# A gated recurrence followed by a PReLU network: attention rebuilt with two batches a step and two masked score products

## The chip, the cores and the metric

The kernel runs on one core of one Trainium2 chip. A core has a matrix engine (PE, which loads a stationary operand, PEld, and streams a moving one past it), a vector engine (DVE), an activation engine (ACT), a general engine (POOL), and a queue for transfers (SP); ACT can issue transfers too. Operands lie in on-chip memory (SBUF, 128 partitions), matrix results in PSUM (128 partitions, eight banks of 512 float32 words each). The metric is the device time of one execution in microseconds (us), the median of the runs shown.

## What is computed

Four batches, eight heads, 768 tokens, 48 dimensions a head. A state of 48 x 48 per head decays by a gate for each key dimension and takes in an outer product at each token; the query reads it. The result, with heads side by side (3072 tokens x 384), goes through a network with 2048 hidden units. Everything is float32; the weights arrive as float64.

```python
f = 1.0 / (1.0 + np.exp(-f_logit))
for t in range(S):
    state = f[:, :, t, :, None] * state + np.einsum('bhd,bhe->bhde', k[:, :, t], v[:, :, t])
    y[:, :, t] = np.einsum('bhd,bhde->bhe', q[:, :, t], state)
x = y.transpose(0, 2, 1, 3).reshape(B * S, H * D)
h = x @ w_in
out = (np.maximum(h, 0.0) + alpha * np.minimum(h, 0.0)) @ w_out
```

## The kernel before

The recurrence is worked in chunks of C = 128 tokens of one batch: 4 x 6 = 24 calls of `attention`. A head's dimensions lie on partitions, two heads at 0 and 64 ("par" 0 and 1), four such pairs (HP) beside each other, tokens along the free dimension. Loads of f, q, k and v have three buffers each (L117, L120).

Within a chunk the scores between tokens s and t need q and k with the product of the gates between them. The kernel goes through seven levels (half sizes h = 1 to 64, the loop at L130). At each, VectorE forms G[h]: k of the lower half of each block with the gates up to the block's border (L139), q of the upper half with the gates from the border on (L134), and doubles the running products R and P (L140, L142). `ks` (L153), transposed on PE (pk, L156) and copied by ACT (L158), times V gives the chunk's share of the next state (pd, L163; L172 and L174).

The levels 64 and 32 are whole blocks of scores (pb, L183 and L189), copied by ACT into the score matrix AT. The six others (MASKED: 16, 8, 4, 2, 1 and the diagonal) are computed as whole 32 x 32 diagonal blocks, six products for each of four blocks and eight heads, 192 matmuls a chunk (pa, L208). VectorE multiplies them by masks (pr, L212), POOL adds the six up (sm, L217 and L218, AT, L221). py (L228) is AT by V; L235 adds qs by the old state. ACT copies py to x (L238), PE transposes it (px, L242), ACT copies it into xT (L244).

After each second chunk `network` is called for the pair before: xT is 256 tokens wide. For each of eight pairs of 128 hidden units six matmuls fill one bank (ph, L254, two "net" banks); ACT makes relu(h) and relu(-h) (L259, L260), VectorE joins them with alpha into g (L263, twelve buffers). Then 16 matmuls for each 128 tokens make po (L269), which VectorE copies to o (L272) and SP stores (L274). A float32 matmul shows as two records of PE and two of PEld, a transpose as one.

`load_weights` turns float64 words into float32 on VectorE, seven operations on each of 16 pieces of 384 words (three buffers, transfers on ACT's queue) of w_in and as many of w_out, between the first calls of `attention`.

The program is unrolled; the order on each engine comes from a planner that lists operations by their place in the program and by estimated times. Each engine then keeps its listed order and waits on semaphores. A buffer that a later tile reuses makes its writer wait for the last reader.

Of the kernel before, what the change touches and what calls it, by code (L numbers as in the profile page):

```python
# [14 lines left out]
WP = 384   # weights of a piece, on each partition  # L15
C = 128   # tokens of a chunk
DB = 32   # diagonal blocks whose levels are cut out by masks
MASKED = (16, 8, 4, 2, 1, 0)   # half sizes of these levels; 0 is the diagonal itself
# [3 lines left out]
def kernel(  # L22
# [32 lines left out]
    T = 2 * C   # tokens of a step of the network  # L55
    NG = len(MASKED) // 2
# [3 lines left out]
    ps2 = ctx.enter_context(tc.tile_pool(name="ps2", bufs=2, space=bass.MemoryType.PSUM))  # L60
    ps1 = ctx.enter_context(tc.tile_pool(name="ps1", bufs=2, space=bass.MemoryType.PSUM))

    def pair(name):
        return ps2.tile([128, 2, 512], F32, tag="pair", name=name)

    def bank(name, tag="att"):
        return ps1.tile([128, 512], F32, tag=tag, name=name)
# [3 lines left out]
    msk = const.tile([128, 2, NG * DB], F32, tag="msk", name="msk")  # L71
    nalpha = const.tile([128, NF], F32, tag="nalpha", name="nalpha")
# [3 lines left out]
    nc.scalar.dma_start(out=msk, in_=masks)  # L76
    nc.scalar.dma_start(out=nalpha, in_=alpha)
    nc.vector.tensor_scalar(nalpha, nalpha, -1.0, None, ALU.mult)

    def load_weights(dst, src, name):  # L80
        """float64 words to float32: mantissa times power of two, each with its bits put together."""
        flat = dst.rearrange("p a n -> p (a n)")
        for n in range(0, flat.shape[1], WP):
            raw = work.tile([128, WP, 2], I32, tag="pr", name=f"{name}_raw{n}", bufs=3)
# [3 lines left out]
            # Mantissa: one and its upper 20 bits as an integer, and the lower 32 behind them.  # L88
            mi = work.tile([128, WP], I32, tag="pos", name=f"{name}_mi{n}")
# [3 lines left out]
            # Exponent: from 11 bits to 8. What float32 can't hold becomes zero or infinite.  # L93
            e = work.tile([128, WP], I32, tag="neg", name=f"{name}_e{n}")
# [6 lines left out]
    # Scores of a chunk, tokens s on partitions, t along the free dimension. What lies under the  # L101
    # diagonal stays zero.
    AT = [const.tile([128, 2, HP, C], F32, tag=f"AT{i}", name=f"AT{i}") for i in range(2)]
    for t in AT:
        nc.gpsimd.memset(t, 0.0)

# [3 lines left out]
    def halves(t, h):  # L110
        return t.rearrange("p a (n two h) -> p (a n) two h", two=2, h=h)

    def attention(b, c, state, xT):
        i = f"{b}_{c}"
        ld = {}
        for nm, src in (("f", fT), ("q", qT), ("k", kT)):
            ld[nm] = work.tile([128, HP, C], F32, tag=nm, name=f"{nm}_{i}", bufs=3)  # L117
            nc.sync.dma_start(out=ld[nm], in_=src[b, c])
        q, k = ld["q"], ld["k"]
        vt = work.tile([128, DM], F32, tag="v", name=f"v_{i}", bufs=3)  # L120
        nc.sync.dma_start(out=vt, in_=v[b, c])

        P = work.tile([128, HP, C], F32, tag="P", name=f"P_{i}")
        nc.scalar.activation(P, ld["f"], AF.Sigmoid)
        R = work.tile([128, HP, C], F32, tag="R", name=f"R_{i}")
        nc.gpsimd.memset(R, 1.0)  # L126

        G = {}
        h = 1
        while h < C:  # L130
            G[h] = work.tile([128, HP, C], F32, tag=f"G{h}", name=f"G{h}_{i}")
            g, qh, kh, p, r = (halves(x, h) for x in (G[h], q, k, P, R))
            n = HP * C // (2 * h)
            nc.vector.tensor_tensor(g[:, :, 1], qh[:, :, 1], p[:, :, 1], ALU.mult)  # L134
            if h == 1:
                nc.scalar.copy(g[:, :, 0], kh[:, :, 0])
                nc.scalar.copy(r[:, :, 0], p[:, :, 1])  # L137
            else:
                nc.vector.tensor_tensor(g[:, :, 0], kh[:, :, 0], r[:, :, 0], ALU.mult)  # L139
                nc.vector.tensor_tensor(  # L140
                    r[:, :, 0], r[:, :, 0], p[:, :, 1, h - 1:h].broadcast_to((128, n, h)), ALU.mult)
            nc.vector.tensor_tensor(  # L142
                p[:, :, 1], p[:, :, 1], p[:, :, 0, h - 1:h].broadcast_to((128, n, h)), ALU.mult)
            h *= 2
        qs = work.tile([128, HP, C], F32, tag="qs", name=f"qs_{i}")
        nc.vector.tensor_tensor(qs, q, P, ALU.mult)

        # The chunk's share of the state behind it: k with the decay to the chunk's end, by V.
        last = c == NC - 1
        new_state = None  # L150
        if not last:
            ks = work.tile([128, HP, C], F32, tag="ks", name=f"ks_{i}")
            nc.vector.tensor_tensor(ks, k, R, ALU.mult)  # L153
            pk = bank(f"pk_{i}")
            for hp in range(HP):
                nc.tensor.transpose(pk[:, hp * 128:(hp + 1) * 128], ks[:, hp], ident)  # L156
            ksn = work.tile([128, HP, 128], F32, tag="ksn", name=f"ksn_{i}")
            nc.scalar.copy(ksn.rearrange("p a d -> p (a d)"), pk)  # L158
            pd = bank(f"pd_{i}")
            for hp in range(HP):  # L160
                for par in range(2):
                    hd = 2 * hp + par
                    nc.tensor.matmul(  # L163
                        pd[64 * par:64 * par + 64, hp * D:(hp + 1) * D],
                        lhsT=ksn[:, hp, 64 * par:64 * par + 64], rhs=vt[:, hd * D:(hd + 1) * D],
                        start=True, stop=True)
# [74 lines left out]
        for kt in range(NK):  # L241
            nc.tensor.transpose(px[:, kt * 128:(kt + 1) * 128], x[:, kt * 128:(kt + 1) * 128], ident)  # L242
# [52 lines left out]
def _level_masks():  # L295
# [4 lines left out]
    per = []  # L300
# [46 lines left out]
```

## Time and profile before

| quantity | us |
|---|---|
| median of 3 runs (1087.6 to 1100.94) | 1090.46 |
| span of the profiled execution, first to last instruction | 1085.6 |
| lowest run, the nearest that is given to the profiled execution's own time | 1087.6 |
| PE busy / PEld busy | 828.5 / 644.5 |
| DVE busy | 572.1 |
| ACT busy / POOL busy | 202.3 / 159.8 |

The span is 2.0 us under the lowest run and 4.9 us under the median. Busy times of engines overlap, so they don't add up to the span; a matmul's end is modelled, and records of PE overlap each other. The granted clock of PE, mean 0.817 of full speed, changes between stretches of the run. "Idle before, releaser" names what ended an engine's idle time; "issue" is time in which an engine waited for nothing that the profile shows.

### The profile page before, as it was taken

To read this page: it belongs to the slowest core of one execution; us is meant where nothing else is said; L and a number is where in the kernel's file an instruction comes from. 1 tells how busy PE (TensorE), PEld (TensorE's weight loads), DVE (VectorE), ACT (ScalarE), POOL (GpSimd) and SP (SyncE) were. 2 spreads that over 40 slices of the span, in tenths; PEclk is the share of its full clock that TensorE was granted. 3 is DMA by queue.
4 is the path that set the end of the run, shared out by engine and by line. 5 is a ranking of instruction groups with operands and counts; after the bars stand their busy time and mean duration, and the time that the engine had idled before them with its cause. 6 is when DMAs were issued, how large, how long until landed. Compare 5 with 4: busy or idle time off the path is not lost.

```text
span 1085.6 us, 29482 instructions
## 1 busy us (share of the span) xinstructions
PE 828.5 (76%) x13464; PEld 644.5 (59%) x13464; DVE 572.1 (53%) x1193; ACT 202.3 (19%) x405; POOL 159.8 (15%) x176
## 2 busy tenths in 40 slices
PE   2504067977977977977977977977986986987998
PEld 1404056666666666656656666756755755856775
DVE  6897997567167157166257256338337437411221
ACT  2100022112122122112122111202211211201220
POOL 1203013022022022022022022013013013003000
PEclk9955576977987977976986966976986986897999
DMA  4452511111011011011011011011011010000000
GB/s 143 126 165 83 156 31 39 35 37 38 8 47 38 8 46 39 18 36 39 8 46 38 8 46 39 10 36 39 8 37 29 8 36 10 1 17 2 1 16 15
DMA packets 22301, 42.90 MB, mean 40 GB/s; under 512 B 2592, under 2 KB 8864, under 8 KB 22176
## 3 DMA queue, kind: packets, MB, share of 16 engines
q1 hardware_dynamic: 17280, 28.32, 8.5%
q10 hardware_dynamic: 4896, 12.69, 4.0%
q8 instruction: 106, 1.74, 0.7%
q14 instruction: 19, 0.16, 0.0%
HBM read 36.28 MB, written 4.72 MB: 38 GB/s over the span
## 4 chain that ended last, share of the span: by engine, by line
PE 61%; POOL 12%; issue 12%; DVE 11%; DMA 2%; ACT 1%; POOLq 0%; DVEq 0%; ACTq 0%
PE po L269 23%; PE ph L254 17%; PE pa L208 8%; POOL AT L221 6%; PE py L228 4%; POOL sm L217 4%; PE py L235 2%; DVE pr L212 2%; POOL sm L218 2%; PE px L242 1%; PE pd L163 1%; PE pb L183 1%; PE pk L156 1%; PE pb L189 1%; DVE P L142 1%
## 5 line engine op out<-in xcount | busy, mean ns | idle before, releaser
L254 PE MATMUL ph<-xT,w_in_sb 128*128 128x256 f32 x1152 | 320.0, 444 | 32.5 <-ACT neg L260 30.8
L254 PEld LDWEIGHTS ph<-xT,w_in_sb 128*128 128x128 f32 x1152 | 257.1, 228 | 79.5 <-ACT neg L260 31.2
L269 PE MATMUL po<-w_out_sb,g 128*128 128x384 f32 x768 | 249.6, 486 | 0.0
L269 PEld LDWEIGHTS po<-w_out_sb,g 128*128 128x128 f32 x768 | 145.9, 190 | 99.2
L263 DVE SCALAR_TENSOR_TENSOR g<-neg,nalpha,pos 128x256 f32<-128x256 f32 x192 | 96.1, 539 | 118.6 <-ACT neg L260 118.6
L208 PE MATMUL pa<-G 48*32 48x32 f32 x7680 | 91.0, 227 | 87.1 <-issue 86.8
L208 PEld LDWEIGHTS pa<-G 48*32 48x32 f32 x7680 | 82.5, 124 | 92.7 <-issue 92.1
L217 POOL TENSOR_TENSOR sm<-pr,pr 128x768 f32<-128x768 f32 x24 | 49.2, 2050 | 578.9 <-DVE pr L212 578.9
L272 DVE COPY o<-po 128x384 f32<-128x384 f32 x24 | 13.4, 558 | 210.0 <-PE po L269 210.0
L228 PE MATMUL py<-v,AT 128*128 128x48 f32 x384 | 51.7, 291 | 87.9 <-POOL AT L221 87.9
L259 ACT ACTIVATE pos<-ph 128x512 f32<-128x512 f32 x96 | 57.3, 597 | 294.0 <-issue 131.4
L228 PEld LDWEIGHTS py<-v,AT 128*128 128x128 f32 x384 | 48.6, 205 | 97.0 <-POOL AT L221 97.0
L142 DVE TENSOR_TENSOR P<-P 128x256 f32<-128x256 f32 x168 | 98.9, 590 | 5.6 <-ACT R L137 1.5
L134 DVE TENSOR_TENSOR G<-q,P 128x256 f32<-128x256 f32 x168 | 80.9, 481 | 28.8 <-PE pa L208 24.1
L212 DVE TENSOR_TENSOR pr<-pa,msk 128x768 f32<-128x768 f32 x48 | 45.9, 956 | 82.9 <-PE pa L208 82.8
L139 DVE TENSOR_TENSOR G<-k,R 128x256 f32<-128x256 f32 x144 | 77.6, 539 | 13.6 <-PE pa L208 8.9
L221 POOL TENSOR_TENSOR AT<-sm 32x256 f32<-32x256 f32 x96 | 76.6, 798 | 6.1
L140 DVE TENSOR_TENSOR R<-R,P 128x256 f32<-128x256 f32 x144 | 73.6, 513 | 0.3
L260 ACT ACTIVATE neg<-ph 128x512 f32<-128x512 f32 x96 | 56.9, 593 | 0.0
L126 POOL MEMSET R<- 128x512 f32 x24 | 12.6, 529 | 255.5 <-DVE ks L153 224.6
L158 ACT COPY ksn<-pk 128x512 f32<-128x512 f32 x20 | 11.7, 586 | 199.0 <-PE pk L156 199.0
L238 ACT COPY x<-py 128x384 f32<-128x384 f32 x24 | 11.5, 479 | 177.2 <-PE py L235 109.3
(49 smaller groups left out, 512.3 us busy)
## 6 DMA issues: line engine op xcount, KB each, us to landing
f<-in_fT SPq DMA_DIRECT2D x24, 256.0 KB, 2.8
q<-in_qT SPq DMA_DIRECT2D x24, 256.0 KB, 3.1
k<-in_kT SPq DMA_DIRECT2D x24, 256.0 KB, 3.8
w_in_raw<-in_w_in ACTq DMA_DIRECT2D x16, 384.0 KB, 3.2
w_out_raw<-in_w_out ACTq DMA_DIRECT2D x16, 384.0 KB, 3.3
v<-in_v SPq DMA_DIRECT2D x24, 192.0 KB, 2.3
out<-o SPq DMA_DIRECT2D x24, 192.0 KB, 1.9
msk<-in_masks ACTq DMA_DIRECT2D x1, 96.0 KB, 3.3
```

The source lines that it names most:

```text
L134: nc.vector.tensor_tensor(g[:, :, 1], qh[:, :, 1], p[:, :, 1], ALU.mult)
L139: nc.vector.tensor_tensor(g[:, :, 0], kh[:, :, 0], r[:, :, 0], ALU.mult)
L140: nc.vector.tensor_tensor(r[:, :, 0], r[:, :, 0], p[:, :, 1, h - 1:h].broadcast_to((128, n, h)), ALU.mult)
L142: nc.vector.tensor_tensor(p[:, :, 1], p[:, :, 1], p[:, :, 0, h - 1:h].broadcast_to((128, n, h)), ALU.mult)
L208: nc.tensor.matmul(pa[j:j + DB, par, col:col + DB], lhsT=lo[r_, hp, j:j + DB], rhs=up[r_, hp, j:j + DB], start=True, stop=True)
L212: nc.vector.tensor_tensor(pr, pa[:, :, 0:HP * NG * DB].rearrange("s r (a x) -> s r a x", a=HP), msk[:, m].unsqueeze(1).unsqueeze(1).broadc ...
L217: nc.gpsimd.tensor_tensor(sm, prods[0], prods[1], ALU.add)
L221: nc.gpsimd.tensor_tensor(A[s_, :, :, s_], sm[s_, :, :, 0:DB], sm[s_, :, :, 2 * DB:3 * DB], ALU.add)
L228: nc.tensor.matmul(py[:, par, hp * D:(hp + 1) * D], lhsT=A[:, par, hp], rhs=vt[:, hd * D:(hd + 1) * D], start=(hp == 0), stop=(state is None),
L254: nc.tensor.matmul(ph[:, j * T:(j + 1) * T], lhsT=w_in_sb[:, kt, (f + j) * 128:(f + j + 1) * 128], rhs=xT[:, kt], start=(kt == 0), stop=(k ...
L263: nc.vector.scalar_tensor_tensor(g[:, j], neg[:, j], nalpha[:, f + j:f + j + 1], pos[:, j], ALU.mult, ALU.add)
L269: nc.tensor.matmul(po[:, 0:DM], lhsT=gs[f // 2][:, f % 2, s * C:(s + 1) * C], rhs=w_out_sb[:, f], start=(f == 0), stop=(f == NF - 1))
```

## The change

`attention(bp, c, ...)` now takes the same 128 tokens of two batches (U = 2), so there are 12 calls, each followed by the network of the step before; one step is W = 1024 words on a partition. The order over the sequence is chunk by chunk, with two pairs of batches in turn. The network's 256 tokens are two batches' 128.

- Gates are grouped by four tokens ("quads"): `kr` holds the products behind a token to its quad's end, `fq` a quad's product, `qd` four copies of q moved on by 0 to 3 gates. `k4` is k with kr; `us` holds q with the gates from its quad's start, and with one to six whole quads more (116 columns for each block of 32 tokens).
- Scores inside a block of 32 need two products only: k by the four rows of qd (`raw`, distances 0 to 3) and k4 by us (`qu`, quads apart). VectorE picks the wanted entries out of PSUM with `copy_predicated`, four and seven for each batch, into `ad`. The mask products (pr) and POOL's sums over six levels (sm) are gone.
- POOL doubles the products over the eight quads of a block (`pre`, `suf`), VectorE makes `q3`, `ks`, `kh` from them. Between the two blocks of a half chunk there is one score product (`off`).
- States are kept every CH = 64 tokens: two shares `pd` and two updates a step; the second product of py reads the state of its half.
- py has dimensions on partitions (V stationary, scores moving). ACT copies it to y, and ten transfers from SBUF to SBUF on SP's queue put the heads' rows into xT. The transposes px are gone.
- The network has four banks; relu(h) is gone (om = 1 - alpha, h read from PSUM by VectorE); ACT copies o; g has ten buffers.
- Weights come in 24 pieces of 512 words with two buffers.
- qd, kr, pre, ad and A are single tiles; k4, us and ksn have one buffer; f, k, v have two. PSUM for attention is two slots of two banks, shared by raw, qu, off, pk, pd and py.

```diff
+        f = quads(load("f", fT))
+        nc.scalar.activation(f, f, AF.Sigmoid)
+        qdv = [qd[:, d * W:(d + 1) * W] for d in range(4)]
+        nc.sync.dma_start(out=qdv[0].rearrange("p (u x) -> p u x", u=U), ...)
...
+        nc.scalar.copy(kr[:, :, 2:3], f[:, :, 3:4])
+        nc.vector.tensor_tensor(kr[:, :, 1:2], f[:, :, 2:3], f[:, :, 3:4], ALU.mult)
+        nc.vector.tensor_tensor(kr[:, :, 0:1], f[:, :, 1:2], kr[:, :, 1:2], ALU.mult)
+        nc.vector.tensor_tensor(fqf, f[:, :, 0:1], kr[:, :, 0:1], ALU.mult)
+        for d in range(1, 4):
+            nc.vector.tensor_tensor(quads(qdv[d])[:, :, d:4], quads(qdv[d - 1])[:, :, d:4],
+                                    f[:, :, 1:5 - d], ALU.mult)
...
+        nc.vector.tensor_tensor(q4, skew..., f[:, :, 0:1]..., ALU.mult)
+        nc.vector.tensor_tensor(k4, k, kr.rearrange("p n r -> p (n r)"), ALU.mult)
+        for m in range(2, NB):
+            nc.vector.tensor_tensor(us[...m...], us[...m - 1...], fq[:, :, 1:1 + n]..., ALU.mult)
+        nc.gpsimd.memset(suf, 1.0)
+        nc.gpsimd.tensor_copy(pin, fq)
+        while h < NB:
+            for n in range(0, NB, 2 * h):
+                nc.gpsimd.tensor_tensor(suf[:, :, lo], suf[:, :, lo], pin[...], ALU.mult)
+                nc.gpsimd.tensor_tensor(pin[:, :, up], pin[:, :, up], pin[...], ALU.mult)
...
+        for u in range(U):
+            raw = pair(f"raw{u}_{i}")
+            for hp in range(HP):
+                for j in range(NJ):
+                    for par in range(2):
+                        nc.tensor.matmul(raw[DB * j:DB * (j + 1), par, hp * C:(hp + 1) * C],
+                                         lhsT=k[r_, g:g + DB], rhs=qd[r_, 0:4 * W]...[:, :, g:g + DB], ...)
+            for d in range(4):
+                nc.vector.copy_predicated(adu, mraw[:, d]..., rv[:, :, d])
+            qu = pair(f"qu{u}_{i}")
+            ... matmul(qu[DB * j:DB * (j + 1), par, hp * UW:(hp + 1) * UW], lhsT=k4[...], rhs=us[r_, g])
+            for m in range(1, NB):
+                nc.vector.copy_predicated(ad[:, u, :, :, 4 * m:DB], mquad[...]..., qu[...])
...
+                        nc.tensor.matmul(pd[64 * par:64 * par + 64, cc, o:o + D], lhsT=ksn[s_, u, ...],
+                                         rhs=vt[s_, u, hd * D:(hd + 1) * D], start=True, stop=True)
...
+                    nc.tensor.matmul(py[64 * par:64 * par + 64, u, hp * C:(hp + 1) * C],
+                                     lhsT=vt[:, u, hd * D:hd * D + 64], rhs=A[:, u, par * HP + hp], ...)
...
+                        nc.tensor.matmul(py[64 * par:64 * par + D, u, o:o + CH],
+                                         lhsT=states[cc][r_, u * HP + hp], rhs=qs[r_, u, hp, cc, 0:CH], ...)
...
+                nc.sync.dma_start(
+                    out=xT[d % 128:d % 128 + n, d // 128].rearrange("p (u t) -> p u t", u=U),
+                    in_=y[p0:p0 + n, :, hd // 2])
...
-            nc.scalar.activation(pos, phv, AF.Relu)
             nc.scalar.activation(neg, phv, AF.Relu, scale=-1.0)
-                nc.vector.scalar_tensor_tensor(g[:, j], neg[:, j], nalpha[:, f + j:f + j + 1], pos[:, j],
+                nc.vector.scalar_tensor_tensor(g[:, j], neg[:, j], om[:, f + j:f + j + 1], phv[:, j],
...
+    for c in range(NC):
+        for bp in range(B // U):
+            state[bp] = attention(bp, c, state[bp], xT)
+            if c == 0:
+                load_weights((w_in_sb, w_out_sb)[bp], (w_in, w_out)[bp], ("w_in", "w_out")[bp])
+            if todo is not None:
+                network(*todo)
+            todo = (bp, c, xT)
+    network(*todo)
```

More of the change, by code (lines that the diff above doesn't have):

```diff
@@ L13 @@
 ALU = mybir.AluOpType
-WP = 384
 C = 128
 DB = 32
-MASKED = (16, 8, 4, 2, 1, 0)
+MASKED = (1, 0)
+U = 2
+CH = 64
+NC2 = C // CH
+NB = DB // 4
+WP = 512
 @with_exitstack
@@ L231, in attention @@
-        if state is not None:
-            for hp in range(HP):
-                for par in range(2):
-                    r_ = rows(par)
-                    nc.tensor.matmul(py[:, par, hp * D:(hp + 1) * D], lhsT=qs[r_, hp], rhs=state[r_, hp],
-                                     start=False, stop=True, skip_group_check=True)
-        x = work.tile([128, DM], F32, tag="x", name=f"x_{i}")
-        nc.scalar.copy(x.rearrange("t (a r d) -> t r a d", r=2, d=D),
-                       py[:, :, 0:HP * D].rearrange("t r (a d) -> t r a d", d=D))
```

363 lines of the change are left out of this document (210 added, 153 removed).

## The prediction

> **What bounds the kernel now.** I read the page's busy table and slices first, then the chain that ended last, then what PE waited for, then one period in order of time.
>
> ```profile
> span 1085.6 us, 29482 instructions
> ...
> PE 828.5 (76%) x13464; PEld 644.5 (59%) x13464; DVE 572.1 (53%) x1193; ACT 202.3 (19%) x405; POOL 159.8 (15%) x176
> ...
> PE   2504067977977977977977977977986986987998
> ...
> PEclk9955576977987977976986966976986986897999
> ...
> PE 61%; POOL 12%; issue 12%; DVE 11%; DMA 2%; ACT 1%; POOLq 0%; DVEq 0%; ACTq 0%
> ...
> q8 instruction: 106, 1.74, 0.7%
> ```
>
> After a start of some five slices the pattern 9-7-7 repeats: a full stretch of network, then two attention chunks with PE two thirds busy and a lower granted clock. The chain runs through PE for 61%, POOL 12%, DVE 11%, and 12% is "issue". PE's waits, then the first and last long products of the timeline:
>
> ```profile
> PE pa L208 <- issue: 109.5, 54, 3.1
> ...
> PE py L228 <- POOL AT L221: 87.9, 23, 37.6
> ...
> 197.97 20.80 PE L269 MATMUL po<-w_out_sb,g 128*128 128x384 f32 x64
> ...
> 1019.99 20.80 PE L269 MATMUL po<-w_out_sb,g 128*128 128x384 f32 x64
> ...
> 198.00:1020.00 822.00, 687.54 (x11214) 534.10 (x11213) 398.15 (x769) 163.35 (x328) 126.39 (x137) 0.83 0.09 26
> ...
> 464.00:546.00 82.00, 26.20 (x96) 21.12 (x96) 8.80 (x16) 0.83 0.10 27
> ```
>
> The first po starts at 197.97, the eleventh at 1019.99: ten periods, 822.0/10 = 82.2 us each. The last row is ph alone in one period: 26.2 us; po takes 20.8. So the network costs PE 47.0 of 82.2 us, and two chunks of attention the other 35.2. After the eleventh po starts, 1085.6 - 1020.0 = 65.6 us remain (po, ph, po, a store). Span = 198.0 + 822.0 + 65.6.
>
> In a chunk (timeline rows):
>
> ```profile
> 469.44 1.33 PE L208 MATMUL pa<-G 48*32 48x32 f32 x127 [2.15 <-issue]
> ...
> 473.27 0.44 PE L208 MATMUL pa<-G 48*32 48x32 f32 x24 [2.49 <-issue]
> ...
> 474.34 5.31 PE L254 MATMUL ph<-xT,w_in_sb 128*128 128x256 f32 x16
> ...
> 476.09 1.92 POOL L217 TENSOR_TENSOR sm<-pr,pr 128x768 f32<-128x768 f32 x1 [42.01 <-DVE pr L212]
> ...
> 478.95 3.38 POOL L221 TENSOR_TENSOR AT<-sm 32x256 f32<-32x256 f32 x4
> ...
> 482.38 1.99 PE L228 MATMUL py<-v,AT 128*128 128x48 f32 x16 [2.73 <-POOL AT L221]
> ```
>
> pa runs in bursts of 127 records and stops 2 us for "issue". 127 matmuls with their weight loads are about 254 instructions; queue q8 brought 106 packets for 2 x 13464 PE records, 254 a packet. So PE ran out of instructions, and a packet lasts 473.27 - 469.44 = 3.83 us. Then POOL's sums take 482.3 - 476.1 = 6.2 us, and py waits.
>
> **The change part by part.** Prices from timeline rows and groups:
>
> ```profile
> 429.48 13.29 PE L254 MATMUL ph<-xT,w_in_sb 128*128 128x256 f32 x60
> ...
> 465.38 0.46 PE L189 MATMUL pb<-G 48*32 48x32 f32 x32
> ...
> 463.24 0.60 PE L156 MATMUL pk<-ident,ks 128*128 128x128 f32 x4
> ...
> 464.51 0.67 PE L163 MATMUL pd<-v,ksn 128*64 128x48 f32 x16 [0.18 <-ACT ksn L158]
> ...
> 485.12 0.42 DVE L140 TENSOR_TENSOR R<-R,P 128x256 f32<-128x256 f32 x1
> ...
> 485.57 0.42 DVE L142 TENSOR_TENSOR P<-P 128x256 f32<-128x256 f32 x1
> ...
> 479.08 0.94 DVE L134 TENSOR_TENSOR G<-q,P 128x256 f32<-128x256 f32 x1
> ...
> 443.97 0.88 DVE L263 SCALAR_TENSOR_TENSOR g<-neg,nalpha,pos 128x256 f32<-128x256 f32 x2 [1.76 <-ACT neg L260]
> ...
> L221 POOL TENSOR_TENSOR AT<-sm 32x256 f32<-32x256 f32 x96 | 76.6, 798 | 6.1
> ...
> L260 ACT ACTIVATE neg<-ph 128x512 f32<-128x512 f32 x96 | 56.9, 593 | 0.0
> ...
> L146 DVE TENSOR_TENSOR qs<-q,P 128x512 f32<-128x512 f32 x24 | 16.4, 684 | 0.4
> ```
>
> *Scores on PE.* Out: pa with 768 records in two chunks, its issue stops, pb, px. In, per step: raw 128 records of 128 columns, qu 128 of 116, off 64 of 32. Not in the trace is a 32-column stationary with so long a moving operand. From below: po streams 384 columns in 20.80/64 = 325 ns, 0.85 ns a column, so 128 columns alone take 108 ns; pa's 10.5 ns a record (1.33 us/127) is less than 32 x 0.85 = 27, so records for different partitions of operands and output overlap; raw has the same eight places as pa, and 108/8 = 13.6 ns. From above: pa's 10.5 for 32 columns, times four, 42 ns. I take 25 ns, near the middle, as the rows fix neither end: raw 128 x 25 = 3.2 us (1.7 to 5.4), qu 2.9 (1.6 to 4.9). off as pb, 0.46/32 = 14 ns: 0.9.
>
> The Trainium skill ("TensorE: Matmul & The Clock Gate", Part 3) has packed tiles span one matmul plus about 4 ns for each further tile; as an estimate that is 108 + 28 = 136 ns for eight, 17 ns each, raw 2.2 and qu 2.0 us, a sum 19 us lower over ten periods. No row here has that shape.
>
> *States and output on PE.* pk 8 transposes at 0.60/4 = 150 ns: 1.2. pd 64 records, pd's row 0.67/16 = 42 ns: 2.7 (half that if its two row halves overlap). py 32 records of 128 columns: 54 ns where the two column groups overlap, 124 as today's py (1.99/16): I take 90, 2.9. State part 64 records of 64 columns, 27 to 54 ns: 40, 2.6. Sum of attention on PE: 3.2 + 2.9 + 0.9 + 1.2 + 2.7 + 2.9 + 2.6 = 16.4 us (10.5 to 21), against 35.2 with waits.
>
> Both row halves of that state part write the same bank, where today's L235 uses two. The Trainium skill ("TensorEngine Tiling (Array Packing)", Gotcha 1) says row tiles cannot use one bank at the same time; by that the part costs 64 x 54 = 3.5 us, 9 us more over ten periods. No row shows it.
>
> *Instructions.* About 240 matmuls x 4 + 16 = 976 per step, plus 320 of the network, 1296 where there were some 2250; at 3.83 us for 254, 976 need 14.7 us, within the time that attention takes anyway. I leave 1 us of issue stops of the 9 to 10 that a period has.
>
> *Getting scores out.* copy_predicated isn't in the trace. L146 takes 684 ns for 512 words, L140 0.42 us for 256: 1.03 ns a word. L140 and L142 start 0.45 us apart, 0.27 for the words and 0.18 fixed; L263's pair takes 0.88 us. Eleven copies for each batch read 1920 words: 22 x 0.18 + 3840 x 1.03 ns = 8.0 us a step. From above POOL's 798 ns for 256 words (L221) gives 22 x 0.80 = 17.6; from below nothing excludes half, 4. PE sees it through the two PSUM slots: raw1 waits for raw0's copies, qu1 for qu0's, then off, pk, pd, py in turn. ACT follows with ten copies, six of 512 words at 0.6 (L260) and four of 256, taken as 0.4: 5.2. PE can run ph in the gaps, as x16 does today (5.31 us beside POOL's sums), now with four banks to run ahead into. I put 3 us a step unfilled (0 to 14, the latter all of it bare). Stops together: 4 us.
>
> *VectorE.* Preparation: 768 (kr, fq) + 1536 (qd) + 2048 (q4, k4) + 2688 (us) + 2048 + 1040 (q3, kh, ks, f64) words in 20 operations = 10.4 + 3.6 = 14.0 us. Copies 8.0, states 1536 words in four, 2.3, network 16 x 0.44 = 7.0: 31.4 us. POOL's 14 small products and a copy take some 5 us, and beside POOL VectorE's product took 0.94 instead of 0.42: 34 at worst 37. Under 65, so it doesn't bound; its cover is PE's network. The loop through single qd is q's load, preparation, raw: about 25 us, also inside.
>
> *Network.* The relu(h) goes from ACT, 0.6 us of each ph, off the path. ph between 96 x 13.29/60 = 21.3 and 26.2: I take 24.5, as fewer small products means less time at the low clock. po 20.8. The o copy on ACT is as long.
>
> *Output by DMA.* ACT's y copies (1.2 us), ten issues and their landing replace px and a copy. The nearest rows:
>
> ```profile
> q<-in_qT SPq DMA_DIRECT2D x24, 256.0 KB, 3.1
> ...
> out<-o SPq DMA_DIRECT2D x24, 192.0 KB, 1.9
> ...
> 453.70 10.66 SPq L274 DMA_DIRECT2D out<-o  x2
> ...
> 474.44 0.34 SPq L118 DMA_DIRECT2D q<-in_qT  x1
> ...
> 474.83 1.35 SPq L118 DMA_DIRECT2D k<-in_kT  x1
> ```
>
> Ten issues at 0.34 to 1.35 and 2 us of landing are 5 to 16 us. Behind them on SP stand the next loads and stores; xT is wanted only after the next attention, some 45 us later. Cost nothing; without that cover, 16 us a period.
>
> *Start.* Rows of weight pieces:
>
> ```profile
> 73.00 0.35 DVE L90 TENSOR_SCALAR w_in_mi<-w_in_raw 128x384 int32<-128x384 int32 x1
> ...
> 75.48 0.35 DVE L90 TENSOR_SCALAR w_in_mi<-w_in_raw 128x384 int32<-128x384 int32 x1
> ...
> 140.83 0.55 DVE L99 SCALAR_TENSOR_TENSOR w_out_sb<-w_out_mi,w_out_e 128x384 f32<-128x384 f32 x1
> ...
> L105 POOL MEMSET AT<- 128x1024 f32 x2 | 1.9, 954 | 0.0
> ...
> 105.33 0.36 DVE L90 TENSOR_SCALAR w_out_mi<-w_out_raw 128x384 int32<-128x384 int32 x1 [6.02 <-DMA w_out_raw<-in_w_out]
> ...
> w_in_raw<-in_w_in ACTq DMA_DIRECT2D x16, 384.0 KB, 3.2
> ```
>
> A piece takes 2.48 us, one of 512 words 3.1; its load about 4. With two buffers (3.1 + 4)/2 = 3.6, times 24 = 86 us. Two attentions 2 x 24.4 = 49, a later beginning behind POOL's memsets (qd's 4100 words alone four times L105's 954 ns) 8, a gap as today's longest 6.0 and a little more, 7: weights done at 150 (140.8 today). The first po no longer waits for two more chunks but for the rest of ph, 12 us: 162 (150 to 180).
>
> *Sum.* Period 24.5 + 20.8 + 16.4 + 4 = 65.7 us. Span 162 + 657 + 65.6 = 885; with the 4.9 us by which the median stood above the profiled span, **890**.
>
> **The rivals.**
> *Well filled.* ph 21.3, attention 12.5, stops 1: period 55.6, 162 + 556 + 70.5 = 789. For: four banks, few issue stops. Against: clock falls in each chunk today.
> *Bare chain.* The planner misjudges the copies and PE waits bare through VectorE's 8.0, ACT's 5.2 and the state's 2 (15 in place of 4, with ph at 26.2): 47.0 + 16.4 + 15 = 78.4, 162 + 784 + 70.5 = 1017. For: today's py waits for POOL in 23 of 24 chunks. Against: ph is there to fill.
> *Loads behind the store (slower).* SP keeps order: above, the store sits 10.66 us until po ends, and q follows. If q's load for the next step, which needs the single qd, is listed behind the stores, then PE ends the network with nothing prepared: load 3.1, sigmoid 1.2 (twice L260's 593 ns for twice the words), preparation 14.0, POOL 5 = 23 us bare a period, 88.7, 162 + 887 + 70.5 = 1120. It needs over 18 bare us to reach "no change", 22 to be slower. Against: qd is free once raw is done, long before po ends, so a planner lists it first.
> *The score copies don't pay.* If copies cost 17.6 us and more, VectorE is at 44, still under PE: this alone gives at most 10 us a period, inside the bare chain.
>
> **How the numbers follow.** Forecast (830 to 950) 0.52; well filled 0.13; bare chain (950 to 1050) 0.22; loads behind the store 0.13, of which 0.04 lands within 2% (about what a measurement of this kernel tells from no change) and 0.09 above. Faster by over 2%: 0.52 + 0.13 + 0.22 = 0.87; same 0.04; slower 0.09. The range 800 to 1015 leaves out the last rival, about 0.03 of the bare chain and 0.04 of the filled one: 0.2.
>
> **What would show it.** Right: a period near 65 us between po's; raw and qu near 25 ns a record; issue stops below 20 us in all; PE waiting on DVE ad or ACT A a few us a step; first po near 160. Wrong: copy_predicated far above 0.45 us for 256 words, PE waiting on DVE qd or q's load at the end of each po, ph waiting on the xT transfers, or a clock so low in attention that ph stays above 26 us.

## The result, and the profile after

| | before | after |
|---|---|---|
| median of 4 runs, us | 1089.15 (1087.6 to 1100.94) | 831.71 (828.53 to 833.33) |
| ratio, 95% interval | | 0.765 [0.760, 0.770] |
| span of the profiled execution, us | 1085.6 | 830.8 |
| first po / second po starts, us | 197.97 / 279.13 | 199.61 / 240.97 |
| period, mean of the nine from the second po to the eleventh, us | 82.32 | 58.25 |
| from the eleventh po to the end, us | 65.6 | 65.6 |

The forecast was 890 with a range of 800 to 1015. The time lies in the range, 58 us under the forecast. Of the runs further on, one (half the products) was in a slower state of the chip for its profile (span 954.9 us) and for two of its four times, so its ratio is taken from the other two, of which the lowest is 939.94 us, and its period, read from that profile, is if anything too long.

The page of the changed kernel, the lines that answer to those shown of before:

```profile
span 830.8 us, 17617 instructions
...
PE 676.2 (81%) x7712; PEld 508.8 (61%) x7712; DVE 429.2 (52%) x920; ACT 159.9 (19%) x289; POOL 81.8 (10%) x228
...
PE   0365453309999998999999999979979979989998
...
PEclk9995675558999999998998999989989999999999
...
q8 instruction: 61, 1.00, 0.5%
...
PE 67%; DVE 20%; DMA 4%; ACT 3%; issue 2%; POOL 2%; SPq 1%; ACTq 0%; DVEq 0%; POOLq 0%
...
L250 DVE COPY_PREDICATED ad<-mraw,raw 128x256 f32<-128x256 int32 x96 | 42.5, 443 | 164.5 <-PE raw L243 161.5
```

The 9-7-7 pattern is gone: from the tenth slice on PE is at 9 tenths, but for three slices at 7 and three at 8. POOL went from 12% of the chain to 2%, "issue" from 12% to 2%, and the instruction packets from 106 to 61. What is left to see is the start: nine slices with PE a third busy, in which DVE is the 20% of the chain.

Nine periods of each kernel by windows: the window, its length, busy time (records) of PE, PEld, DVE, ACT and POOL, granted clock, DMA share and GB/s. The second row is ph alone (a row leaves out engines without work on that tile). Before:

```profile
279.13:1019.99 740.86, 621.24 (x10099) 482.78 (x10098) 349.11 (x670) 146.97 (x295) 113.00 (x122) 0.82 0.09 25
...
279.13:1019.99 740.86, 243.68 (x865) 194.88 (x864) 79.19 (x144) 0.82 0.09 25
```

After:

```profile
240.97:765.21 524.24, 492.58 (x5731) 369.34 (x5730) 245.89 (x533) 114.25 (x211) 33.32 (x118) 0.96 0.14 41
...
240.97:765.21 524.24, 207.11 (x865) 166.87 (x864) 62.54 (x144) 43.00 (x72) 0.96 0.14 41
```

Divided by nine, with po at 20.80 in both, a period becomes:

| us per period | before | after | difference |
|---|---|---|---|
| ph | 27.08 | 23.01 | -4.1 |
| other work of PE (attention) | 21.15 | 10.92 | -10.2 |
| PE idle | 13.29 | 3.52 | -9.8 |
| sum with po | 82.32 | 58.25 | -24.1 |

Nine such gains are 217 us; the second po, 38 us earlier, makes up the rest of 255. Two fifths of a period's gain are work that PE no longer has, two fifths are waits, and a sixth is ph itself, at a granted clock of 0.96 in place of 0.82.

One period of the changed kernel, PE's timeline (start, length, what, records, and in brackets the idle time before it with what ended it):

```profile
410.71 20.80 PE L378 MATMUL po<-w_out_sb,g 128*128 128x384 f32 x64
431.44 1.16 PE L243 MATMUL raw<-qd,k 48*32 48x128 f32 x64
432.34 1.07 PE L259 MATMUL qu<-us,k 48*32 48x116 f32 x64
434.68 1.15 PE L243 MATMUL raw<-qd,k 48*32 48x128 f32 x64 [1.27 <-DVE ad L250]
435.76 0.70 PE L364 MATMUL ph<-xT,w_in_sb 128*128 128x256 f32 x2
437.09 1.80 PE L259 MATMUL qu<-us,k 48*32 48x116 f32 x64 [0.63 <-DVE ad L264]
...
445.55 1.15 PE L296 MATMUL pd<-v,ksn 64*64 64x48 f32 x64
...
449.14 1.97 PE L329 MATMUL py<-A,v 128*64 128x128 f32 x32
451.04 1.99 PE L340 MATMUL py<-q,state 48*48 48x64 f32 x64
452.96 15.81 PE L364 MATMUL ph<-xT,w_in_sb 128*128 128x256 f32 x72
```

Each attention product takes 1 to 2 us. The bare waits stand where the two PSUM slots change hands: raw1 waits for raw0's copies, qu1 for qu0's. After po comes no ph at first, then only 2 records between raw1 and qu1. (The last row's 72 records of ph, and rows of 6 to 10 left out above, make up the rest of it.)

The waits of PE in the whole run (us in all, times, longest) show what the periods no longer hold, and what the start does:

```profile
PE qu L259 <- DVE w_out_sb L143: 29.0, 1, 29.0
...
PE ph L364 <- DVE w_in_sb L143: 24.9, 4, 15.0
...
PE raw L243 <- DVE qd L181: 20.0, 1, 20.0
...
PE qu L259 <- DVE ad L264: 15.0, 11, 5.5
...
PE raw L243 <- DVE ad L250: 11.9, 9, 1.8
...
PE off L276 <- issue: 8.3, 3, 3.2
```

The three longest happen once or a few times, in the start. The py that waited 87.9 us for POOL and the pa that waited 109.5 for instructions are not there.

### The profile page after: what moved, and what is told of

Read it like the earlier page. It is cut to its first block, busy times and chain, and to the rows that moved or that the text cites. A ratio compares the mean times of both kernels' runs of the same rounds, so it can differ in the third digit from the quotient of the medians.

```text
span 830.8 us, 17617 instructions
## 1 busy us (share of the span) xinstructions
PE 676.2 (81%) x7712; PEld 508.8 (61%) x7712; DVE 429.2 (52%) x920; ACT 159.9 (19%) x289; POOL 81.8 (10%) x228
## 4 chain that ended last, share of the span: by engine, by line
PE 67%; DVE 20%; DMA 4%; ACT 3%; issue 2%; POOL 2%; SPq 1%; ACTq 0%; DVEq 0%; POOLq 0%
PE po L378 30%; PE ph L364 27%; DVE ad L264 4%; DVE ad L250 3%; PE py L329 3%; PE py L340 2%; ACT A L316 2%; DMA w_in_raw<-in_w_in 2%; SPq L351 1%; DVE us L186 1%; DMA w_out_raw<-in_w_out 1%; PE pk L284 1%; DVE us L195 1%; PE qu L259 1%; PE raw L243 1%
## 5 line engine op out<-in xcount | busy, mean ns | idle before, releaser
L364 PE MATMUL ph<-xT,w_in_sb 128*128 128x256 f32 x1152 | 276.9, 398 | 26.3 <-DVE w_in_sb L143 24.9
L364 PEld LDWEIGHTS ph<-xT,w_in_sb 128*128 128x128 f32 x1152 | 224.8, 199 | 62.6 <-DVE w_in_sb L143 26.4
L372 DVE SCALAR_TENSOR_TENSOR g<-neg,om,ph 128x256 f32<-128x256 f32 x192 | 83.3, 476 | 133.1 <-ACT neg L369 132.6
L250 DVE COPY_PREDICATED ad<-mraw,raw 128x256 f32<-128x256 int32 x96 | 42.5, 443 | 164.5 <-PE raw L243 161.5
L259 PE MATMUL qu<-us,k 48*32 48x116 f32 x1536 | 32.5, 305 | 52.2 <-DVE w_out_sb L143 29.0
L264 DVE COPY_PREDICATED ad<-mquad,qu 128x224 f32<-128x224 int32 (+6 forms) x168 | 49.8, 296 | 24.8 <-PE qu L259 21.2
L243 PE MATMUL raw<-qd,k 48*32 48x128 f32 x1536 | 30.4, 290 | 34.1 <-DVE qd L181 20.0
L195 DVE TENSOR_TENSOR us<-us,fq 128x768 f32<-128x768 f32 (+2 forms) x72 | 44.5, 617 | 0.0
L316 ACT COPY A<-ad 32x512 f32<-32x512 f32 x48 | 29.6, 616 | 19.3 <-DVE ad L264 18.9
L209 POOL TENSOR_TENSOR suf<-suf,pre 128x32 f32<-128x32 f32 (+2 forms) x84 | 29.9, 382 | 1.8
```

What stands on the lines that cost most here:

```text
L195: nc.vector.tensor_tensor(us[:, :, UO[m]:UO[m] + 4 * n].rearrange("p g (i r) -> p g i r", r=4), us[:, :, skip:skip + 4 * n].rearrange("p g ...
L209: nc.gpsimd.tensor_tensor(suf[:, :, lo], suf[:, :, lo], pin[:, :, n + 2 * h - 1:n + 2 * h].broadcast_to((128, G, h)), ALU.mult)
L243: nc.tensor.matmul(raw[DB * j:DB * (j + 1), par, hp * C:(hp + 1) * C], lhsT=k[r_, g:g + DB], rhs=qd[r_, 0:4 * W].rearrange("p (d x) -> p d ...
L250: nc.vector.copy_predicated(adu, mraw[:, d].rearrange("p i r -> p (i r)").bitcast(I32).unsqueeze(1).broadcast_to((128, H, DB)), rv[:, :, d])
L259: nc.tensor.matmul(qu[DB * j:DB * (j + 1), par, hp * UW:(hp + 1) * UW], lhsT=k4[r_, g * DB:(g + 1) * DB], rhs=us[r_, g], start=True, stop= ...
L264: nc.vector.copy_predicated(ad[:, u, :, :, 4 * m:DB], mquad[:, lo:lo + n].bitcast(I32).unsqueeze(1).unsqueeze(1).broadcast_to((128, 2, HP, ...
```

## The experiments

Spans are given for the part of the time that a window shows; ratios are against the kernel before, run beside each; its medians there go from 1088.6 to 1101.3 us. "Other PE" is PE's work without ph and po.

| run | median, us | ratio [interval] | 2nd po | period | ph | other PE | PE idle | clock |
|---|---|---|---|---|---|---|---|---|
| before | 1089.15 | | 279.13 | 82.32 | 27.08 | 21.15 | 13.29 | 0.82 |
| after | 831.71 | 0.765 [0.760, 0.770] | 240.97 | 58.25 | 23.01 | 10.92 | 3.52 | 0.96 |
| half the products | 953.09 | 0.867 [0.858, 0.876] | 254.78 | 70.47 | 25.95 | 16.74 | 6.97 | 0.87 |
| short sums | 1016.12 | 0.933 [0.928, 0.938] | 266.25 | 75.78 | 25.47 | 19.36 | 10.14 | 0.86 |
| copies twice | 820.71 | 0.753 [0.750, 0.757] | 244.27 | 56.63 | 22.24 | 10.67 | 2.92 | 0.99 |
| one place | 907.92 | 0.833 [0.829, 0.837] | 255.29 | 64.96 | 21.90 | 20.58 | 1.68 | 1.00 |
| transposes | 848.64 | 0.775 [0.768, 0.781] | 235.19 | 60.80 | 23.17 | 12.89 | 3.94 | 0.98 |
| ph between | 788.94 | 0.725 [0.720, 0.731] | 239.33 | 53.53 | 22.49 | 9.63 | 0.60 | 1.00 |
| weights in 3 | 800.70 | 0.729 [0.723, 0.735] | 212.30 | 57.91 | 22.88 | 10.94 | 3.30 | 0.96 |
| ph between, copies twice | 817.18 | 0.750 [0.746, 0.754] | 244.58 | 56.26 | 22.25 | 10.21 | 3.00 | 1.00 |
| ph between, weights in 3 | 757.26 | 0.695 [0.692, 0.699] | 211.23 | 53.21 | 22.45 | 9.46 | 0.50 | 1.00 |

**Two parts of the gain, made in the kernel before.** First half of the products (b1): one group of three levels in place of two. The matmuls of the other group, their instructions and one of VectorE's two mask products a chunk go.

```diff
-        for m in range(2):
+        for m in range(1):
...
-        nc.gpsimd.tensor_tensor(sm, prods[0], prods[1], ALU.add)
+        nc.gpsimd.tensor_tensor(sm, prods[0], prods[0], ALU.add)
```

> Kernel before, with the second group of products (levels 2, 1 and the diagonal) and its mask product left out; POOL adds the first group to itself, so its work stays. Theory (attention before is bound by PE records and the instructions that they need): 384 records a period less, 768 instructions at 3.83 us per 254 = 11.6 us, at least half of pa's 9.1 us busy and 9.2 us stopped; ten periods 90 to 115 us, time 970 to 1000 us. Rival (POOL's sums end every chunk whatever PE does): only the mask product leaves the chain, 2 x 0.96 us a period, 1060 to 1075 us.

The ratio puts it 13% under the kernel before, further than I expected, and the period shrank by 11.9 us: 4.4 of PE's work, 6.3 of idle time, 1.1 of ph. The products of one period by PE's timeline, of its first chunk with the py behind them, and the last of its second:

```profile
490.90 1.84 PE L208 MATMUL pa<-G 48*32 48x32 f32 x192
...
501.81 3.65 PE L228 MATMUL py<-v,AT 128*128 128x48 f32 x16 [5.41 <-POOL AT L221]
...
514.12 0.43 PE L208 MATMUL pa<-G 48*32 48x32 f32 x22 [1.99 <-issue]
```

In the first chunk all 192 records run without the two "issue" stops of 2 us that stood in them before; the second keeps one. PE's waits for issue at that line fell from 109.5 to 36.5 us in the run, and in the nine periods from 80.2 to 27.7. POOL's sums stayed: its busy time in the nine periods went only from 113.0 to 106.7 us, and py's wait for them from 35.9 to 32.5. The period fell all the same, by nearly half of the change's 24.1. So the rival that the sums alone end the chunk falls; products with their instructions set it too. The run takes out both at once, so it doesn't price a record's work and its instructions apart.

Then POOL's sums (b2): two of the four additions are left out.

```diff
-        nc.gpsimd.tensor_tensor(sm, prods[0], prods[1], ALU.add)
-        nc.gpsimd.tensor_tensor(sm[:, :, :, 0:DB], sm[:, :, :, 0:DB], sm[:, :, :, DB:2 * DB], ALU.add)
...
-            ...(A[s_, :, :, s_], sm[s_, :, :, 0:DB], sm[s_, :, :, 2 * DB:3 * DB], ALU.add)
+            ...(A[s_, :, :, s_], prods[0][s_, :, :, 0:DB], prods[1][s_, :, :, 2 * DB:3 * DB], ALU.add)
```

> Kernel before, with POOL's first two additions left out (four of six levels are missing from the scores); the four additions into AT stay. Theory (py's wait of 1.9 us a chunk in the steady part is what is left bare of POOL's 6.2 us, ph covers the rest): POOL's chain gets 2.8 us shorter, py's wait goes, at most 3.9 us a period and some at the start: 1035 to 1060 us. Rival (ph only fills what would otherwise run later, so nothing is gained): 1080 to 1092 us. Second rival (all of POOL's chain is bare): 24 x 2.8 = 68 us less, 1020 us.

72 us went, more than I expected: 6.5 of a period, half of them idle time, the rest PE's own rows. Here the other wait moved: in nine periods py's wait for POOL fell from 35.9 to 6.7 us, and the stops for issue stayed (80.2 and 81.2). I had taken the ph beside the sums for useful cover. The kernel before put 16 records there in 5.31 us, 332 ns each, at a granted clock of 0.69, where 60 in a row take 221 at 0.99; the shorter sums leave room for 12, and py waits 0.5 us in place of 2.7:

```profile
448.91 4.70 PE L251 MATMUL ph<-xT,w_in_sb 128*128 128x256 f32 x12
454.14 1.99 PE L225 MATMUL py<-v,AT 128*128 128x48 f32 x16 [0.52 <-POOL AT L218]
```

These 12 take 392 ns each, at a granted clock of 0.60. Work put beside a wait ran at a lowered clock there, so the gap was not filled at full value, and over all the periods the clock rose from 0.82 to 0.86 with the shorter sums. That fits the 1.6 us that ph lost a period; how much of the other rows' 1.8 is the clock was not measured apart. The sums had cost more than the wait that stands behind them.

**The price of the score copies (a1).** The changed kernel with each copy_predicated made twice, by the prediction's price 8 us a step more of VectorE.

```diff
-            for d in range(4):
+            for d in (0, 0, 1, 1, 2, 2, 3, 3):
...
-            for m in range(1, NB):
+            for m in [m for m in range(1, NB) for _ in range(2)]:
```

> Changed kernel with each of the 22 copies of scores made twice (same result), 8 us of VectorE more a step. Theory (PE runs ph in these gaps): 0 to 3 us a period, 832 to 870 us. Rival (the chain of copies lies bare on the path): 8 us a step more, 12 x 8 = 96, 920 to 930 us.

I expected no gain, and it is faster than the changed kernel, 0.753 against 0.765, with intervals that don't meet. VectorE's busy time rose by 5.6 us a period (296.38 us in nine) and the period fell by 1.6. PE's timeline says why:

```profile
436.88 1.07 PE L259 MATMUL qu<-us,k 48*32 48x116 f32 x64
437.88 2.43 PE L364 MATMUL ph<-xT,w_in_sb 128*128 128x256 f32 x10
441.13 1.15 PE L243 MATMUL raw<-qd,k 48*32 48x128 f32 x64 [0.83 <-DVE ad L250]
442.21 5.02 PE L364 MATMUL ph<-xT,w_in_sb 128*128 128x256 f32 x22
```

32 records of ph stand between qu0 and qu1, where the changed kernel has 2: the planner, which goes by estimated times, gave longer copies more to do beside them. If the order of the list is what gained here, and not the copies, it should gain without them. The next run sets that order by hand.

**The order of ph (c1), and the copies again (c3).** The network's ph tiles are written as a call that makes one of eight, and attention calls it after raw1, qu0, qu1, off, pk and twice after pd.

```diff
+            if u == 1:
+                fill()
...
+    def hidden(bp, c, xT):
+        def one():
+            f = 2 * len(gs)
...
-            state[bp] = attention(bp, c, state[bp], xT)
+            h = hidden(*todo) if todo is not None else None
+            early = h is not None and c > 0
+            state[bp] = attention(bp, c, state[bp], xT, h[1] if early else (lambda: None))
```

> Changed kernel with the eight ph tiles of the step before written between the products of attention (one after each of raw1, qu0, qu1, off and pk, two after pd), so that PE's list has six matmuls of ph wherever it waits for copies. Theory (the doubled copies were faster because the planner then puts more of ph into the gaps; PE idles 3.5 us a period and ph runs at a lowered clock after it): idle under 1 us and ph 22 us, period 54 to 55.5 us, time 790 to 805 us. Rival (it was not the order on PE): 824 to 836 us.

```profile
421.64 1.07 PE L261 MATMUL qu<-us,k 48*32 48x116 f32 x64
422.65 2.86 PE L376 MATMUL ph<-xT,w_in_sb 128*128 128x256 f32 x12
425.43 1.16 PE L243 MATMUL raw<-qd,k 48*32 48x128 f32 x64
426.52 2.86 PE L376 MATMUL ph<-xT,w_in_sb 128*128 128x256 f32 x12
429.31 1.09 PE L261 MATMUL qu<-us,k 48*32 48x116 f32 x64
...
441.14 1.17 PE L301 MATMUL pd<-v,ksn 64*64 64x48 f32 x64 [1.01 <-ACT ksn L291]
```

The brackets of raw and qu are empty, idle time goes from 3.52 to 0.60 us a period, ph and attention each speed up a little at a granted clock of 1.00, and 43 us go: a little more than I expected. The changed kernel's stops came from the order in which ph was listed. With this order and doubled copies:

> The same with each copy of scores made twice. Theory (order on PE): with the order fixed the copies can only cost; 0 to 20 us over the run with single copies. Rival (doubled copies help by themselves): 8 us or more under it, as 820.7 against 831.7.

817.18 us, 0.750 [0.746, 0.754]: 28 above the run with single copies, where I expected at most 20. The profiled spans are 30 apart: 9 x 2.73 = 25 in the periods (56.26) and 5 in the start. So doubled copies gain nothing in themselves; they end at nearly the same period (56.63 and 56.26) whether ph is listed by hand or not. In the changed kernel the single copies hide once ph is between them; with twice the time they don't.

**How the small products share PE (a5, a10).** First the records of raw and qu in another order: four matmuls of one place in PE (the same partitions of operands and of output) one after the other, where neighbours differed in place. raw's loop, and qu's is changed the same way:

```diff
-            for hp in range(HP):
-                for j in range(NJ):
-                    for par in range(2):
+            for par in range(2):
+                for j in range(NJ):
+                    for hp in range(HP):
```

> Changed kernel with raw and qu in another order: four matmuls in a row use the same rows of operands and the same output partitions. Theory (a record costs about 14 ns only because neighbours use eight different places and overlap): one alone is 108 ns, so raw and qu grow from 4.6 to 15 to 28 us a step, partly under the copies; 930 to 1080 us. Rival (records overlap in any order, or the issue of instructions sets 14 ns): 828 to 840 us.

```profile
401.67 4.00 PE L243 MATMUL raw<-qd,k 48*32 48x128 f32 x61
```

65.6 ns a record, where eight places in turn take 1.16/64 = 18. The overlap is real and worth 9.7 us of PE's work a period. But one record alone costs 66, not the 108 that I had worked out from po, so the time is under my 930.

In the other direction, py, whose two halves write one bank; here each half of a pair writes another (both products of py; ACT then copies four half tiles):

```diff
-                    nc.tensor.matmul(py[64 * par:64 * par + 64, u, hp * C:(hp + 1) * C],
+                    nc.tensor.matmul(py[64 * par:64 * par + 64, u ^ par, hp * C:(hp + 1) * C],
```

> The changed kernel, but the products of py for par 0 and par 1 write two different PSUM banks at a time instead of one (and ACT copies py in four half copies instead of two). In the changed kernel 64 records of the state part take 1.99 us and 32 of the scores by V 1.97 us, which is 31 ns for 64 columns and 62 for 128, just what 0.49 ns a column (62.7 ns for 128 in the run with all records at one place) gives one after the other. Theory that the one bank keeps the two halves apart: state part near 1.0 us, scores by V near 1.0 if its two column groups can overlap at all; PE's other work falls by 1 to 2 us a period and the time by 5 to 18 us, ACT's two more copies off the path. Rival, that the bank has nothing to do with it and the small products have a price of their own: both rows stay at 1.9 to 2.0 us, time within 5 us of 832, or a few us above by ACT's copies.

```profile
448.71 1.97 PE L329 MATMUL py<-A,v 128*64 128x128 f32 x32
450.61 1.99 PE L340 MATMUL py<-q,state 48*48 48x64 f32 x64
```

Both rows are what they were, and the time is 830.3 us, 0.758 [0.752, 0.763], no different. So one bank for both halves is not what sets these rows. Why 64 columns take 31 ns and 128 take 62 stays open: it is what 0.49 ns a column gives one after the other, and also what two halves at once take at twice that.

**The output by dimension (a3).** py, the copy and px as in the kernel before, for each of the two batches; the DMAs into xT are out.

```diff
-                nc.sync.dma_start(out=xT[d % 128:d % 128 + n, d // 128]..., in_=y[p0:p0 + n, :, hd // 2])
+            for kt in range(NK):
+                nc.tensor.transpose(px[:, 0, kt * 128:(kt + 1) * 128], x[:, kt * 128:(kt + 1) * 128], ident)
+            nc.scalar.copy(xT[:, :, u * C:(u + 1) * C], px[:, 0, 0:NK * 128]...)
```

> Changed kernel with the output part undone: py has tokens on partitions again (scores stationary, 128 columns), ACT copies it to x, PE transposes x, ACT copies into xT; no transfers from SBUF to SBUF. Theory (the transfers are hidden, the gain of this part is PE work): six transposes at 150 ns, 0.9 us, and 32 records of py at 124 instead of 62 ns, 2.0 us, make 2.9 us a step more, 12 x 2.9 = 35 us: 850 to 885 us. Rival (the landing of xT lies on the path): without it the time falls below 825 us.

848.64 us, 17 more than the changed kernel, 1.4 short of what I expected; the ratios' intervals, 0.775 [0.768, 0.781] and 0.765 [0.760, 0.770], touch, so the windows decide. The period grows by 2.55 us, 2.0 of it PE's work: px takes 1.1 us and py 1.8 more, and other small rows a little less. The start is 6 us shorter, and what the transfers have to do with that is open. In the periods the part pays by PE's work; no wait of PE on a transfer shows in the ten-DMA version.

**The PReLU on ACT again (a4).** relu(h) back on ACT, VectorE reads it instead of PSUM.

```diff
+            nc.scalar.activation(g, phv, AF.Relu)
...
-                nc.vector.scalar_tensor_tensor(g[:, j], neg[:, j], om[:, f + j:f + j + 1], phv[:, j],
+                nc.vector.scalar_tensor_tensor(g[:, j], neg[:, j], om[:, f + j:f + j + 1], g[:, j],
```

> Changed kernel with the PReLU part undone: ACT makes relu(h) into g and relu(-h), VectorE adds alpha times the second in place. Theory (ACT is busy a fifth of the time and four banks cover the longer chain of each ph): 826 to 845 us. Rival (the two passes free each bank later and ph waits 0.6 us each): 8 x 0.6 x 12 = 58 us more, 880 to 895 us.

829.08 us, 0.757 [0.751, 0.762], period 58.30: no difference from the changed kernel.

**What bounds the start (a9, a6).** First more loads in flight: pieces of 256 words, ten buffers.

```diff
-WP = 512
+WP = 256
...
-            raw = work.tile([128, WP, 2], I32, tag="y", name=f"{name}_raw{n}")
+            raw = work.tile([128, WP, 2], I32, tag="g", name=f"{name}_raw{n}", bufs=10)
```

> Changed kernel with weights in 48 pieces of 256 words in the ten buffers of g, seven operations each. VectorE's work grows by some 12 us (fixed part of 168 more operations), transfers run far ahead. Theory (VectorE bounds the start): 825 to 848 us. Rival (transfers with two buffers bound it): 800 to 820 us.

834.64 us, 0.762 [0.756, 0.767], the first po at 204.16. VectorE's waits for weight pieces before it went from 8.7 us to 0.3, and its own work, with more and shorter operations, from 168 to 182 us: it is the work, and not the transfers, that the first po follows. Then fewer operations: three in place of seven on each piece, by shifts and masks.

```diff
+            nc.vector.tensor_scalar(e, hi, 3, 0x3FFFFFF8, ALU.logical_shift_left, ALU.bitwise_and)
+            nc.vector.scalar_tensor_tensor(e, lo, 29, e, ALU.logical_shift_right, ALU.bitwise_or)
+            nc.vector.scalar_tensor_tensor(flat[:, n:n + WP].bitcast(I32), hi, -0x40000000, e, ALU.bitwise_and, ALU.bitwise_or)
```

> Changed kernel with three bit operations instead of seven on each piece of weights (cut off instead of rounded to float32, for numbers that float32 holds as normal ones or zero). Theory (the first po is late because VectorE is busy 168 of 199.6 us): start to start 3.1 us of a piece becomes 1.55, 24 x 1.55 = 37 us less: 790 to 805 us. Rival (transfers of pieces with two buffers set the pace, 3.5 us landing each): 815 to 832 us.

Windows of the start, up to the first po, of the changed kernel and, in the second fence, of this one:

```profile
0.00:199.60 199.60, 80.08 (x1598) 66.74 (x1599) 168.36 (x352) 32.60 (x55) 46.78 (x106) 0.73 0.37 118
```

```profile
0.00:170.94 170.94, 83.78 (x1688) 69.47 (x1689) 134.06 (x271) 32.37 (x55) 36.93 (x110) 0.76 0.45 144
```

VectorE is busy 168 of the first 200 us; with 34 us less of it the first po starts 29 us sooner, and the time falls by 31. VectorE's work bounds the start.

**Order and weights together (c2).**

> ph tiles between the products of attention and the weights in three bit operations (cut off instead of rounded). Theory (start and steady part are separate terms): the two gains add, 31 us off the run with ph between: 758 to 775 us. Rival (a shorter start is given back, since the steady part is bound by something else than PE): above 785 us.

757.26 us, 31.7 under the run with the order alone and just under the 758 that I expected at the least: the gains add, and this beats both kernels of the case.

Not tried, and so open: the two batches a step or the states every 64 tokens by themselves, and a second qd.

## Why the prediction was right, and where it was off

**Sum.** The second po, by the forecast's steps at 162 + 65.7 = 227.7, came at 240.97: 13 us late. Nine periods at 58.25 in place of 65.7 took 67 off, the end was the forecast's 65.6. 885 + 13 - 67 = 831. The mechanism was right: small products with their instructions (b1) and POOL's sums (b2) were what the periods lost; the sizes of three terms were off, and the late start hid part of the faster periods. b1's 11.9 us and b2's 6.5 are 18.4 of a period's 24.1; the output by dimension gives 2.6 more (a3), and what is left was not taken apart.

**Attention on PE: 16.4 forecast, 10.9 measured.** This is the largest error. PE's groups in the nine periods (busy us, mean ns of a record with its overlap, idle time before):

```profile
L259 PE MATMUL qu<-us,k 48*32 48x116 f32 x1114 | 21.7, 285 | 6.0 <-DVE ad L264 5.5 <-issue 0.5
L243 PE MATMUL raw<-qd,k 48*32 48x128 f32 x1088 | 20.0, 273 | 10.3 <-DVE ad L250 10.1 <-issue 0.2
...
L340 PE MATMUL py<-q,state 48*48 48x64 f32 x576 | 17.9, 217 | 0.0
L329 PE MATMUL py<-A,v 128*64 128x128 f32 x288 | 17.7, 276 | 3.0 <-ACT A L316 2.6
...
L284 PE MATMUL pk<-ident,ks 128*128 128x128 f32 x72 | 13.2, 342 | 0.4 <-issue 0.4
L296 PE MATMUL pd<-v,ksn 64*64 64x48 f32 x576 | 10.3, 220 | 0.0
L276 PE MATMUL off<-q,kh 48*32 48x32 f32 x576 | 9.2, 219 | 11.9 <-issue 8.3 <-DVE ad L250 3.5
```

A step's 128 records of raw take 2.35 us (3.2 forecast) and of qu 2.5 (2.9); the window holds 8.5 steps of raw and 8.7 of qu. pd takes 1.15 (2.7), py's two parts 4.0 (5.5), pk 1.5 (1.2) and off 1.0 (0.9). These rows overlap, so they add up to more than the 10.9 that PE is busy with them. I had put raw at 25 ns, near the middle between 13.6 and 42; 20.0/1088 is 18. The 42 was four times pa's price, so it took pa's 10.5 ns for the cost of 32 columns, and the upper bound pulled the choice up. pd at 42 ns was pd's old row, of 128 rows; two halves of 64 take 18. The packing figure of the Trainium skill ("TensorE: Matmul & The Clock Gate", Part 3), which gave an estimate of 17 ns for raw, lies beside the trace's 18, but in part by luck: with the 65.6 ns that one record alone takes here, the same rule gives (65.6 + 28)/8 = 12. The rule of the Trainium skill ("TensorEngine Tiling (Array Packing)", Gotcha 1), that row tiles cannot use one bank at the same time, gave an estimate of 3.5 us for the state part; it takes 1.99, and 1.99 with two banks as well, so no run here shows the bank as its limit.

**Network: ph 24.5 forecast, 23.0 measured.** Right in its direction, fewer small products and a higher clock. c1 shows the rest: at a clock of 1.00 it is 22.5.

**Stops: 4 forecast, 3.5 measured.** Here size and place were right, the size in part by luck. By the rows above DVE's ad ended 19.1 us of idle time in the nine periods (2.1 a period), ACT's A 2.6 (0.3), and issue 9.0, the sum of the 1 us a period that I had left. But issue did not come in each period: off was stopped three times, by 2.1 to 3.2 us, in the periods of 61.4, 61.5 and 59.3 us, where the others take 54.6 to 57.9. One of them:

```profile
558.04 0.32 PE L276 MATMUL off<-q,kh 48*32 48x32 f32 x4 [3.09 <-issue]
```

I had feared copies longer than the planner takes them for. c1 shows that another order of ph closes all these stops; whether the planner left ph out of the gaps because it took the copies for shorter is not shown.

**VectorE and copy_predicated.** 443 ns for 256 words, forecast 0.45 us. VectorE has 27.3 us a period (31.4 forecast), so its sum bounds nothing there; what PE waits for are single copies.

**Output by DMA and PReLU.** Costed at nothing, and in the periods so they were: a3's are longer without the DMAs, by 2.0 us of PE's work in px and py, and a4 is the same without the PReLU's change. In the start a3 is 6 us shorter, so there the DMAs may have cost something.

**Start: first po at 162 forecast, 199.6 measured.** This step failed, though its effect on the sum is small. DVE's groups before the first po:

```profile
L264 DVE COPY_PREDICATED ad<-mquad,qu 128x224 f32<-128x224 int32 (+6 forms) x42 | 12.3, 293 | 0.5 <-PE qu L259 0.3
L250 DVE COPY_PREDICATED ad<-mraw,raw 128x256 f32<-128x256 int32 x28 | 12.3, 438 | 1.2 <-ACT y L345 1.1
...
L190 DVE TENSOR_TENSOR k<-k,kr 128x1024 f32<-128x1024 f32 x4 | 5.0, 1260 | 0.0
```

I had counted two attentions between the weights. VectorE did four preparations (one k4 each), three and a half steps of raw's copies (28 at eight each) and three of qu's (42 at fourteen each) before the last weight piece was done at 188.4: two preparations, 12 copies for raw and 14 for qu more. That is 2 x 14.0 us by my own price and 5.3 + 4.1 at the measured 438 and 293 ns, 37 us, where the first po came 38 late. For that PE has no attention between the first and the second po (they stand 41.4 us apart, ph and po alone), so 24 of the 38 us come back at once.

**The rivals.** *Well filled* (789) didn't come by itself, but c1 made its periods: 53.5 for the rival's 55.6, with idle time of 0.6 for its 1. That c1's time is 788.94 as well is luck: its first po came at 198 and not at 162, and its periods are shorter. *Bare chain* falls with a1: 5.6 us more of VectorE's work a period should have stretched it, and it shrank. *Loads behind the store* came true as an order and cost nothing. In the periods SP's queue does send the next q behind the stores:

```profile
421.73 10.68 SPq L383 DMA_DIRECT2D out<-o  x2
435.88 0.39 SPq L164 DMA_DIRECT2D qd<-in_qT  x1
```

But it is the q of the step after: it starts when raw1 ends (435.83, the row at 434.68 above) and so frees the single qd, and the raw that reads it starts at 489.34, a whole period later. PE's one wait for qd, 20.0 us, lies in the start. *The score copies don't pay* needed 0.8 us a copy.

## What to carry to other kernels

Where PE waits behind a chain of small products and masks, count the instructions as well as the busy time: here fewer records removed work, instruction stops and a low clock in one move. After such a change the bound sat here in two places that the change was not about, the order in which long products are listed between the short ones (43 us) and the preparation of data before the first period (31 us); look at both before the new operations. Price a packed small product from a row with the same places, not from its columns and a long product's rate.

## What was unexpected of the hardware

A 128-column record of 48 x 32 alone takes 65.6 ns, 0.51 a column (0.49 in a later burst, 3.07 us for 49), where po's 128 x 128 records take 0.85 a column; no run here says why. In the kernel before, ph runs 221 ns a record when PE is full, at a granted clock of 0.99, and 332 beside POOL's sums, at 0.69. One VectorE operation on 1024 words, us by qd with a skewed read (L186), took 1990 ns, and another on as many words (L190) 1260.
